# A gated delta-rule attention chain and a soft-MoE layer on one core: 64-row and 64-column array tiles, fixed key and query slots, 128-token outputs, a new instruction order

## The chip, the cores and the metric

The kernel runs on one core of one Trainium2 chip. A core has a matrix engine (PE, with weight loads shown apart as PEld), a vector engine (DVE), a scalar engine (ACT), GpSimd (POOL) and a DMA-issuing engine (SP). Each engine works through its own queue in order and waits on semaphores. PE writes to PSUM, which has 8 banks of 512 fp32 columns on 128 partitions; ACT and DVE copy ("evict") results from there to SBUF.

The metric is the device time of one execution in microseconds (us). Before the change it is 337.9 us, the median of three runs (336.04 to 340.29).

## The reference, cut to what matters

```python
# 4 batches x 8 heads, 768 tokens, head size 48
k_n = k / (norm(k) + 1e-06)
for t in range(S):
    y[:, :, t] = einsum('bhd,bhde->bhe', q[:, :, t], state)
    v_old = einsum('bhde,bhd->bhe', state, k_n[:, :, t])
    state = state + beta_t * einsum('bhd,bhe->bhde', k_n[:, :, t], v[:, :, t] - v_old)
x = y.transpose(0, 2, 1, 3).reshape(3072, 384)
logits = x @ phi                       # 32 slots: 8 experts x 4
d = softmax(logits, over tokens)
slot_input = d.T @ x
h = relu(slot_input[e] @ w1[e])        # 384 -> 1024
slot_out[e] = h @ w2[e]                # 1024 -> 384
c = softmax(logits, over slots)
out = c @ slot_out
```

## The kernel before, in words

**Chunks.** The 768 tokens are cut into 12 chunks of 64. The sequential recurrence inside a chunk is replaced by matrix products: with the Gram matrix of the keys, a 64x64 triangular system is inverted for each of the 32 heads, and the state is carried from chunk to chunk. Two batches' halves of the 32 heads sit on partitions 0-63 and 64-127 (index `r`); the 16 heads of a half are 8 pairs `j` with two members `c`.

**Work of one chunk n.** `load` brings K, Q and V (L414), K and V in ten DMAs each, Q in two. K and Q are padded from 48 to 64 columns per head by a memset (L420). `turn` transposes K and Q in 128x128 blocks on PE (L472) and evicts them into `KQ[n]` (L285 on ACT or L287 on DVE, the two copies of the helper `copy`). `prep` multiplies keys with keys and queries, the Gram products (L501, 48 rows contracted, 64x128 out), which are masked and spread (L509, L514, L524, L537). For each pair of chunks `invert` inverts 16x16 diagonal blocks elementwise (L559 to L617, its products and differences L281 on DVE or POOL). For each chunk `join` extends the inverse to 32 and to 64 by four PE products (L671, 64x64 stationary, 16 or 32 moving columns for each j, r) with evictions and corrections between (L681, L687/L689, L698, L708). `step` carries the state: `ks` = keys times state (L759), the difference with the scaled V (L765), `w` = inverse times difference (L776), interleaved with the previous chunk's attention product `mau` (L720), eviction to U, `sup` = state update (L803, accumulated in the fixed two-bank tile `pS`), and its eviction `sev` into the other state buffer (a 48-partition copy for each c, one on ACT, one on DVE, each reading both banks). `query` (L729) applies the old state to the queries. `route` transposes the output (L838); `pair` computes, for two chunks, the logits (L856), running softmax statistics, the slot sums (L891) and the combine weights (L900 to L920).

**After the last chunk** come the merge (L985 to L1009), the expert layers (L1025, L1041, L1058), the slot outputs (L1064, L1065), and the combination with the token weights (L1078): 24 groups of four products, each 64 tokens wide, one 384-column eviction and one 192 KB DMA (L1084) for each group. The weights `w1` and `w2` (25 MB) stream into SBUF during the second half (L964, L975), wherever earlier tiles have become free.

**Order and places.** The order of all operations, the engine of each that has a choice, and the SBUF and PSUM addresses are written out by hand in three tables, `ORDER`, `ALTS` and `PLACE`. They were made by a planner that is not part of the kernel; the durations in the calls of `pl.op` are its inputs and are not used when the kernel is built.

Of the kernel before, what the change touches and what calls it, by code (L numbers as in the profile page):

```python
# [10 lines left out]
AX = mybir.AxisListType  # L11
ALU = mybir.AluOpType
# [60 lines left out]
]  # L73
PLACE = [
# [126 lines left out]
def kernel(  # L201
# [108 lines left out]

    ident = lambda: A(cident)
    col1 = lambda c: A(cm0)[:, c:c + 1]
    M0, M1, NM0, NM1, LO, HI, NLO, NHI = [partial(col1, c) for c in range(8)]
    XMSK = lambda qq: A(cxm)[:, qq:qq + 1]

    pperm = pl.buf(1, psum=True)
# [799 lines left out]
```

## Time and profile before

| | |
|---|---|
| median of three runs | 337.9 us |
| the profiled execution | 337.52 us, of which the span from first to last instruction 335.8 us |
| mean PE clock granted over the span | 0.859 |
| PE idle until the first transposes (L472) | 17.0 us |
| first Gram products (L501) | 22.6 us |
| first spread for the inversion (L559) | 36.0 us |
| first `w` (L776) | 78.6 us |
| first expert product (L1025) | 290.3 us |
| last combination product (L1078) ends | about 327.5 us |
| HBM read, written | 39.5 MB, 4.7 MB |

Times inside a profile count from the first instruction. "x32" behind a PE line counts records: an fp32 matmul leaves two, an fp32 transpose one. The granted clock is a share of full speed; in this trace it is only ever 1.0 or 0.5, and it changes at multiples of 3.41 us from each other.

### The profile page before, as it was taken

How to read it: one execution, taken by the hardware profiler on the slowest of the kernel's cores; microseconds unless marked ns; L12 is line 12 of the kernel's file. 1: busy time of each engine (PE TensorE's matmuls, PEld its weight loads, DVE VectorE, ACT ScalarE, POOL GpSimd, SP SyncE). 2: the span in 40 equal slices, each digit the busy share in tenths (PEclk: the TensorE clock that was granted, in tenths of full speed). 3: DMA queues.
4: the chain of work that ended last, by engine and by line, in shares of the span. 5: the costliest groups of instructions: out<-in, count | busy, mean ns of one | idle time of the engine just before them, and what ended most of it. 6: DMA issues, size and time to landing. Idle time of an engine off the chain costs nothing.

```text
span 335.8 us, 14727 instructions
## 1 busy us (share of the span) xinstructions
PE 271.8 (81%) x6348; PEld 228.4 (68%) x6348; DVE 216.2 (64%) x570; ACT 130.6 (39%) x296; POOL 147.1 (44%) x257
## 2 busy tenths in 40 slices
PE   0086577898968798999899897997879699899990
PEld 0075466788967688888799676787759687336780
DVE  2264898669877585796768878478775465544360
ACT  1025437445615434463652413565433223130132
POOL 7060578134537465126662666272342622160110
PEclk9999658555969996999957998797978979999996
DMA  8976655430016646133111956367395957994287
GB/s 118 139 120 100 101 85 88 69 72 3 8 22 114 120 83 118 27 54 51 33 23 55 188 142 173 103 177 193 97 322 175 322 171 248 356 378 165 74 271 224
DMA packets 77697, 45.16 MB, mean 134 GB/s; under 512 B 60064, under 2 KB 70160, under 8 KB 77632
## 3 DMA queue, kind: packets, MB, share of 16 engines
q1 hardware_dynamic: 66304, 26.49, 34.8%
q0 software_dynamic: 6128, 15.31, 16.8%
q10 hardware_dynamic: 5200, 2.41, 2.8%
q8 instruction: 50, 0.82, 1.0%
q14 instruction: 15, 0.12, 0.1%
HBM read 39.47 MB, written 4.72 MB: 132 GB/s over the span
## 4 chain that ended last, share of the span: by engine, by line
PE 53%; DVE 21%; DMA 8%; issue 7%; ACT 5%; POOL 4%; SPq 1%; DVEq 0%; POOLq 0%; ACTq 0%
PE pb L671 11%; PE pb L501 7%; DVE sb L281 5%; PE pb L472 5%; PE pb L776 4%; PE pb L759 4%; DMA sb<-in_k_dram 4%; PE pb L1058 3%; PE pb L803 3%; PE pb L1025 3%; POOL sb L281 3%; PE pb L729 3%; PE pb L1078 3%; DMA sb<-in_v_dram 2%; PE pb L838 2%
## 5 line engine op out<-in xcount | busy, mean ns | idle before, releaser
L285 ACT ACTIVATE sb<-pb 128x512 f32<-128x512 f32 (+5 forms) x125 | 69.0, 578 | 132.7 <-PE pb L472 38.1
L281 POOL TENSOR_TENSOR sb<-sb 128x256 f32<-128x256 f32 (+10 forms) x108 | 62.6, 587 | 102.3 <-DVE sb L281 46.5
L671 PE MATMUL pb<-sb 64*64 64x16 f32 (+1 forms) x1536 | 62.9, 228 | 7.8 <-DVE sb L287 3.7
L671 PEld LDWEIGHTS pb<-sb 64*64 64x64 f32 x1536 | 59.2, 156 | 14.7 <-issue 8.6
L472 PE MATMUL pb<-sb 128*128 128x128 f32 x192 | 37.7, 350 | 23.7 <-DVE sb L330 17.0
L281 DVE TENSOR_TENSOR sb<-sb 128x120 f32<-128x120 f32 (+9 forms) x137 | 47.6, 351 | 9.8 <-POOL sb L281 4.8
L287 DVE COPY sb<-pb 128x384 f32<-128x384 f32 (+5 forms) x62 | 34.9, 573 | 26.1 <-PE pb L803 5.1
L472 PEld LDWEIGHTS pb<-sb 128*128 128x128 f32 x192 | 28.4, 179 | 28.6 <-issue 20.6
L501 PE MATMUL pb<-sb 48*64 48x128 f32 x768 | 35.0, 332 | 7.4 <-DVE sb L287 2.8
L501 PEld LDWEIGHTS pb<-sb 48*64 48x64 f32 x768 | 29.2, 168 | 10.0 <-ACT sb L285 5.6
L776 PE MATMUL pb<-sb 64*64 64x48 f32 x768 | 28.9, 234 | 4.4 <-DVE sb L765 3.0
L776 PEld LDWEIGHTS pb<-sb 64*64 64x64 f32 x768 | 27.0, 149 | 6.9 <-DVE sb L765 3.1
L720 PE MATMUL pb<-sb 64*64 64x48 f32 x768 | 27.2, 226 | 1.5 <-issue 1.5
L720 PEld LDWEIGHTS pb<-sb 64*64 64x64 f32 x768 | 25.3, 142 | 0.9 <-issue 0.8
L759 PE MATMUL pb<-sb 128*64 128x96 f32 x352 | 20.3, 278 | 3.2 <-DVE sb L287 1.8
L975 POOL DMA_DIRECT2D sb<-in_moe_w_dram x32 | 17.4, 546 | 11.8 <-PE pb L1025 7.7
L509 ACT ACTIVATE sb<-pb,sb 128x128 f32<-128x128 f32 x48 | 16.6, 366 | 15.1 <-DVE sb L537 7.9
L537 DVE TENSOR_TENSOR sb<-pb,sb 128x512 f32<-128x512 f32 x16 | 11.0, 688 | 17.5 <-ACT sb L509 7.7
L759 PEld LDWEIGHTS pb<-sb 128*64 128x64 f32 x352 | 18.2, 160 | 4.8 <-ACT sb L285 2.1
L729 PE MATMUL pb<-sb 128*64 128x96 f32 x352 | 17.6, 255 | 0.4 <-DVE sb L765 0.2
L414 POOL DMA_DIRECT2D sb<-in_k_dram x25 | 13.9, 567 | 8.8 <-DVE sb L429 8.8
L803 PE MATMUL pb<-sb 64*48 64x48 f32 x704 | 13.6, 228 | 4.7 <-issue 3.6
(139 smaller groups left out, 389.0 us busy)
## 6 DMA issues: line engine op xcount, KB each, us to landing
sb<-in_moe_w_dram SPq DMA_DIRECT2D x32, 256.0 KB, 5.1
sb<-in_moe_w_dram POOLq DMA_DIRECT2D x32, 192.0 KB, 5.4
sb<-in_moe_w_dram SPq DMA_DIRECT2D x32, 192.0 KB, 5.1
sb<-in_moe_w_dram POOLq DMA_DIRECT2D x16, 256.0 KB, 5.5
sb<-in_q_dram SPq DMA_DIRECT2D x13, 192.0 KB, 4.3
out_dram<-sb SPq DMA_DIRECT2D x10, 192.0 KB, 2.4
out_dram<-sb ACTq DMA_DIRECT2D x10, 192.0 KB, 3.5
sb<-in_k_dram SPq DMA_DIRECT2D x19, 96.0 KB, 3.5
```

What stands on the lines that cost most here:

```text
L281: ENG[e].tensor_tensor(*a, **kw)
L285: nc.scalar.activation(o, i, ACT.Copy)
L287: V.tensor_copy(o, i)
L472: nc.tensor.transpose(A(ps)[:, 0, P * j:P * j + P], A(src)[:, x:x + P], ident())
L501: mm(A(ps)[ha(r), c, P * j4:P * j4 + P], x[hd(c), j, r, 0:64], x[hd(c), j, r])
L671: mm(A(ps)[ha(r), 0, w * j:w * j + w], stat()[ha(r), 64 * j:64 * j + 64], mov()[ha(r), w * j:w * j + w])
L720: mm(pv(pY)[ha(1 - r), j // 4, j % 4, c], A(at)[ha(r), 512 * c + 64 * j:512 * c + 64 * j + 64], hv(u)[ha(r), j, c], start=first and c == 0 ...
L729: mm(A(pY)[ha(1 - r), j // 4, 96 * (j % 4):96 * (j % 4) + 96], kqv(KQ[n])[:, j, r, 1], Sv(n)[:, j, r], start=j % 4 == 0)
L759: mm(A(pR)[ha(r), j // 4, 96 * (j % 4):96 * (j % 4) + 96], kqv(KQ[n])[:, j, r, 0], Sv(n)[:, j, r])
L776: mm(pv(pW)[ha(r), j // 4, j % 4, c], A(Zs[n])[ha(r), 512 * c + 64 * j:512 * c + 64 * j + 64], hv(R)[ha(r), j, c])
L803: mm(A(pS)[hd(c), r, D * j:D * j + D], hv(Kb[n])[ha(r), j, c], hv(U)[ha(r), j, c], start=n == 0 and j == 0)
L975: ENG[q].dma_start(out=A(t)[:, Dm * x:Dm * x + Dm], in_=s[:, 2 * tp + x])
```

## The change

- `join` (L671): each product streams 64 moving columns in place of 16 or 32, the same columns repeated 4 or 2 times; the result takes 64 columns for each j, and the readers pick the first 16 or 32.
- Gram (L501): 64 rows are contracted in place of 48 (the pads are zero). `sup` (L803): the stationary tile has 64 columns in place of 48. `KQ` keeps keys and queries in two halves.
- K and Q have 8 and 4 fixed slots of 1,024 columns, used in turn. The pads are zeroed once for each slot ahead of the loads (12 memsets) and not for each load (24).
- 11 of the 24 `w1` tiles are placed in K and Q slots that are done with, and one `w2` tile in the last.
- The state is laid out by r first. `sev` copies one bank for each engine, as two 48-partition copies of 384 columns, in place of one 768-column copy that reads both banks.
- `invert`: the norms are three operations with a separate copy of the diagonal; each column step is two operations, product and difference, which may run on different engines.
- `pair`: sums come out of the exponentials (`accum_out`), so three DVE operations for each pair are gone; the exponential of the combine weights is four ACT calls of 32 columns in place of one of 128.
- The combination works on 128 tokens: 12 groups of four products (32 rows, 128 stationary columns, 192 moving), a 768-column eviction, and four 96 KB DMAs for each group.
- `ORDER`, `ALTS` and `PLACE` are new.

```diff
-    def load(src, n, split, pad):
-        W = 64 if pad else D
-        t = pl.buf(16 * W)
+    NK, NQ = 8, 4
+    kslot, qslot = [[fixed(1024) for _ in range(x)] for x in (NK, NQ)]
+    for i in range(NK):
+        pl.tag = ("pad", i)
+        for t in ([kslot[i]] + ([qslot[i]] if i < NQ else [])):
+            pl.op([("POOL", 0.32), ("DVE", 0.28)], None, lambda e, t=t: ENG[e].memset(
+                A(t).rearrange("p (x d) -> p x d", x=16)[:, :, D:], 0.0), w=[t])
...
+    def load(src, n, pad):
+        t = kslot[n % NK] if pad else pl.buf(KW)
...
-        if pad:
-            pl.op([("POOL", 0.32), ("DVE", 0.28)], None, lambda e: ENG[e].memset(
-                A(t).rearrange("p (x d) -> p x d", x=16)[:, :, D:], 0.0), w=[(t, 1)])
...
+    def load_q(n):
+        t = qslot[n % NQ]
...
-    kqv = lambda t: A(t).rearrange("p (j r a t) -> p j r a t", j=8, r=2, a=2)
+    kqv = lambda t: A(t).rearrange("p (a j r t) -> p j r a t", j=8, r=2, a=2)
...
-                            x = A(KQ[n]).rearrange("p (j r f) -> p j r f", j=8, r=2)
-                            mm(A(ps)[ha(r), c, P * j4:P * j4 + P], x[hd(c), j, r, 0:64], x[hd(c), j, r])
+                            x = kqv(KQ[n])
+                            mm(A(ps)[ha(r), c, P * j4:P * j4 + P].rearrange("p (a t) -> p a t", a=2),
+                               x[ha(c), j, r, 0], x[ha(c), j, r])
...
-            def go(e):
-                p = A(pr)[:, 0:n].rearrange("p (x i k) -> p x i k", x=2 * X, k=m)
-                sh = [P, 2 * X, w, m]
-                tt(e, p, blk(tb, j, j + 1, 0, m).broadcast_to(sh),
+            def mul(e):
+                tt(e, p(), blk(tb, j, j + 1, 0, m).broadcast_to(sh),
                    blk(lb, j, j + 1, j + 1, 16).rearrange("p x a i -> p x i a").broadcast_to(sh), op=ALU.mult)
+            pl.op(both, None, mul, r=[lb, tb], w=[pr], dp=True)
+
+            def sub(e):
                 t = blk(tb, j + 1, 16, 0, m)
-                tt(e, t, t, p, op=ALU.subtract)
+                tt(e, t, t, p(), op=ALU.subtract)
+            pl.op(both, None, sub, r=[pr], w=[tb], dp=True)
...
-                        mm(A(ps)[ha(r), 0, w * j:w * j + w], stat()[ha(r), 64 * j:64 * j + 64], mov()[ha(r), w * j:w * j + w])
+                        m = mov()[ha(r), w * j:w * j + w].unsqueeze(1).broadcast_to([64, RJ // w, w])
+                        mm(A(ps)[ha(r), 0, RJ * j:RJ * j + RJ].rearrange("p (a t) -> p a t", t=w), stat()[ha(r), 64 * j:64 * j + 64], m)
...
-                            mm(A(pS)[hd(c), r, D * j:D * j + D], hv(Kb[n])[ha(r), j, c], hv(U)[ha(r), j, c],
+                            mm(A(pS)[ha(c), r, D * j:D * j + D], A(Kb[n]).rearrange("p (j c d) -> p j c d", j=8, c=2)[ha(r), j, c], hv(U)[ha(r), j, c],
...
-            for c in H2:
-                def sev(e, c=c):
-                    o = A(nz).rearrange("p (j r c d) -> p r j c d", j=8, r=2, c=2)[hd(c), :, :, c]
-                    i = A(pS)[hd(c), :, 0:8 * D].rearrange("p r (j d) -> p r j d", d=D)
-                    copy(e, o, i)
+            for r in H2:
+                def sev(e, r=r):
+                    for c in H2:
+                        o = A(nz).rearrange("p (r j c d) -> p r j c d", j=8, r=2, c=2)[hd(c), r, :, c]
+                        copy(e, o, A(pS)[hd(c), r, 0:8 * D].rearrange("p (j d) -> p j d", d=D))
...
-            nc.scalar.activation(A(d), A(Lc), ACT.Exp, bias=A(nm))
+            nc.scalar.activation(A(d), A(Lc), ACT.Exp, bias=A(nm), accum_out=A(ls))
...
+        def ce():
+            for x in range(4):
+                nc.scalar.activation(A(Eg)[:, 32 * x:32 * x + 32], A(pN)[:, 0, 32 * x:32 * x + 32], ACT.Exp,
+                                     bias=A(cmx)[:, x:x + 1], accum_out=A(smv)[:, x:x + 1])
...
+    done = qslot + [kslot[x % NK] for x in (N - 1, *range(N - NK, N - 2))]
...
-            w1b[e, kk] = t = pl.buf(F)
+            w1b[e, kk] = t = done.pop(0) if done else pl.buf(F)
...
+        for g2 in range(NG // 2):
+            for z in H2:
+                po, ob = pl.buf(2, psum=True), pl.buf(2 * Dm)
+
+                def comb(po=po, z=z, g2=g2, so=so):
+                    for x in H2:
+                        for b in H2:
+                            p0 = 32 * (2 * z + b)
+                            g = 2 * g2 + x
+                            mm(A(po)[:, b, HD * x:HD * x + HD], A(cT)[p0:p0 + 32, P * g:P * g + P], A(so)[p0:p0 + 32])
```

More of the change, by code (lines that the diff above doesn't have):

```diff
@@ L163, in buf, with op @@
         return Buf(self, size, **kw)
-    def op(self, eng, dur, fn, r=(), w=(), after=(), bus=0.0, rec=0, hold=(), nd=1, dp=False, skip=None):
+    def op(self, eng, dur, fn, r=(), w=(), after=(), bus=0.0, rec=0, hold=(), nd=1, dp=False, skip=None, act=0):
         o = Op(eng if dur is None else [(eng, dur)], fn if dur is None else (lambda e: fn()))
-        o.nd, o.dp, o.skip = nd, dp, skip
+        o.nd, o.dp, o.skip, o.act = nd, dp, skip, act
         o.src, o.tag, o.bus, o.rec, o.soft = fn, self.tag, bus, rec, [x for x in self.soft if x is not None]
@@ L312 @@
     col1 = lambda c: A(cm0)[:, c:c + 1]
-    M0, M1, NM0, NM1, LO, HI, NLO, NHI = [partial(col1, c) for c in range(8)]
+    M0, M1, NM0, NM1, HI, LO, NHI, NLO = [partial(col1, c) for c in range(8)]
     XMSK = lambda qq: A(cxm)[:, qq:qq + 1]
@@ L399, in load @@
+    def load(src, n, pad):
+        t = kslot[n % NK] if pad else pl.buf(KW)
         s = src.rearrange("b h s d -> s (b h) d")
         d = lambda: A(t).rearrange("p (x d) -> p x d", x=16)[:, :, 0:D]
-        parts = []
         for r in H2:
             h0 = 16 * (1 - r)
-            if not split:
-                parts.append((64 * r, 64, slice(0, 16), n * C, slice(h0, h0 + 16)))
-                continue
-            parts.append((64 * r, 64, slice(0, 16, 2), n * C, slice(h0, h0 + 16, 2)))
+            parts = [(64 * r, 64, slice(0, 16, 2), n * C, slice(h0, h0 + 16, 2))]
@@ L409, in load @@
             for k in range(4):
                 parts.append((64 * r + 16 * k, 16, slice(1, 16, 2), n * C + 48 - 16 * k, slice(h0 + 1, h0 + 16, 2)))
-        def go(ps, e):
-            for p0, w, x, t0, hs in ps:
-                ENG[e].dma_start(out=d()[p0:p0 + w, x], in_=s[t0:t0 + w, hs])
-        h = len(parts) // 2
-        c = (2.6, 2.95, 2.5 if src is k and n < 2 else None) if split else (0.65, 0.86, 0.62 if n < 2 else None)
-        for r, ps in ((0, parts[:h]), (2, parts[h:])):
-            pl.op(dq(*c), None, partial(go, ps), w=[(t, r)], bus=0.0012 * 64 * 8, nd=h)
@@ L419, in load, with go @@
-        if pad:
-            pl.op([("POOL", 0.32), ("DVE", 0.28)], None, lambda e: ENG[e].memset(
-                A(t).rearrange("p (x d) -> p x d", x=16)[:, :, D:], 0.0), w=[(t, 1)])
+            def go(e, ps=parts):
+                for p0, w, x, t0, hs in ps:
+                    ENG[e].dma_start(out=d()[p0:p0 + w, x], in_=s[t0:t0 + w, hs])
+            pl.op(dq(2.6, 2.95, 2.5 if src is k and n < 2 else None), None, go, w=[(t, 2 * r)], bus=1.5, nd=5)
+        return t
+    def load_q(n):
+        t = qslot[n % NQ]
+        s = q.rearrange("b h s d -> s (b h) d")
+        d = lambda: A(t).rearrange("p (x d) -> p x d", x=16)
+        for r in H2:
+            pl.op(dq(0.67, 0.86, 0.75 if n < 2 else None), None, lambda e, r=r: ENG[e].dma_start(
+                out=d()[64 * r:64 * r + 64, :, 0:D], in_=s[n * C:n * C + C, 16 * (1 - r):16 * (2 - r)]), w=[(t, 2 * r)], bus=1.5)
@@ L553, in invert @@
         part = lambda t, i: A(t)[:, GS * i:GS * i + 1024]
-        pl.op(pop(GS * X)[:1], None, lambda e: ENG[e].memset(A(tb), 0.0), w=[tb])
+        pl.op([("POOL", 1.0), ("DVE", 1.05)], None, lambda e: ENG[e].memset(A(tb), 0.0), w=[tb])
         for i, g in enumerate(gs):
@@ L561, in invert, with norm1, norm2 @@
             pl.op("DVE", 1.25, spread, r=[Gd[g]], w=[(lb, i)])
-        y, y1, n4, sq = [pl.buf(32 * X) for _ in range(4)]
+        y, y1, n4, sq, mt = [pl.buf(32 * X) for _ in range(5)]
         dg = lambda t: A(t).rearrange("p (i f) -> p i f", f=GS)[:, :, 0:1024:33]
         v = lambda t: A(t).rearrange("p (i k) -> p i k", k=32)
-        def norms():
-            q = 1.0 - 3.02e-4
+        hq = 1.0 - 3.02e-4
+        def norm1():
             V.tensor_scalar(v(y).bitcast(I32), dg(lb).bitcast(I32), 0.5, float(0x1FBD1DF5), op0=ALU.mult, op1=ALU.add)
             V.reciprocal(A(sq), A(y))
-            V.scalar_tensor_tensor(v(sq), dg(lb), q, v(sq), op0=ALU.mult, op1=ALU.mult)
-            V.scalar_tensor_tensor(A(y1), A(y), q, A(sq), op0=ALU.mult, op1=ALU.add)
+            V.scalar_tensor_tensor(v(sq), dg(lb), hq, v(sq), op0=ALU.mult, op1=ALU.mult)
+            V.scalar_tensor_tensor(A(y1), A(y), hq, A(sq), op0=ALU.mult, op1=ALU.add)
+        pl.op("DVE", 1.02, norm1, r=[lb], w=[y, y1, sq], dp=True)
+        def norm2():
             V.reciprocal(A(sq), A(y1))
@@ L574, in norms, with norm3 @@
             V.scalar_tensor_tensor(A(n4), A(y1), 4e-6, A(sq), op0=ALU.add, op1=ALU.add)
+        pl.op("DVE", 0.82, norm2, r=[lb, y1], w=[n4, sq], dp=True)
+        def norm3():
             V.tensor_tensor(A(sq), A(n4), A(n4), op=ALU.mult)
@@ L577, in norms @@
             g0 = 32 * gs[0]
-            V.tensor_tensor(dg(tb), A(cbb)[:, g0:g0 + 32 * X].rearrange("p (i k) -> p i k", k=32), v(sq), op=ALU.mult)
-        pl.op("DVE", 1.7 if X == 1 else 2.5, norms, r=[lb, cbb], w=[n4, sq, tb, y, y1], dp=True)
+            V.tensor_tensor(A(mt), A(cbb)[:, g0:g0 + 32 * X], A(sq), op=ALU.mult)
+        pl.op("DVE", 0.82, norm3, r=[n4, cbb], w=[sq, mt], dp=True)
+        pl.op([("ACT", 0.22), ("DVE", 0.2), ("POOL", 0.3)], None, lambda e: nc.scalar.activation(dg(tb), v(mt), ACT.Copy) if e == "ACT" else ENG[e].tensor_copy(
+            dg(tb), v(mt)), r=[mt], w=[tb], dp=True)
         def scale(e):
-            o = blk(lb, 0, 16, 0, 16)
-            m = dg(tb).rearrange("p i (x t) -> p (i x) t", x=2) if X == 1 else None
             for i in range(X):
                 o = blk(lb, 0, 16, 0, 16)[:, 2 * i:2 * i + 2]
-                m = part(tb, i)[:, 0:1024:33].rearrange("p (x t) -> p x t", x=2)
+                m = A(mt)[:, 32 * i:32 * i + 32].rearrange("p (x t) -> p x t", x=2)
                 tt(e, o, o, m.unsqueeze(2).broadcast_to([P, 2, 16, 16]), op=ALU.mult)
-        pl.op([("DVE", 0.7 * X - 0.08 * (X - 1))], None, scale, r=[tb], w=[lb], dp=True)
+        pl.op([("DVE", 0.7 * X - 0.08 * (X - 1))], None, scale, r=[mt], w=[lb], dp=True)
         pr = pl.buf(128 * X)
@@ L624, in blocks @@
         return A(b).rearrange("p (s j i c) -> p s c j i", s=2, c=2, j=8)[:, s]
+    RJ = 64
     def join(n):
@@ L659, in mask @@
             return go
-        pl.op([("DVE", 0.78), ("POOL", 1.42), ("ACT", 1.1)], None, mask(Gd[g], s1, True), r=[(Gd[g], 2 * s), (Gd[g], 2 * s + 1), cs1, cm0], w=[s1], dp=True)
-        pl.op([("ACT", 0.88), ("DVE", 0.78), ("POOL", 1.42)], None, mask(td, s2, False), r=[td, cm0], w=[s2], dp=True)
+        pl.op([("DVE", 0.78), ("POOL", 1.45), ("ACT", 1.25)], None, mask(Gd[g], s1, True), r=[(Gd[g], 2 * s), (Gd[g], 2 * s + 1), cs1, cm0], w=[s1], dp=True)
+        pl.op([("ACT", 0.95), ("DVE", 0.55), ("POOL", 1.88)], None, mask(td, s2, False), r=[td, cm0], w=[s2], dp=True)
         def madd(e):
@@ L689, in wide @@
                     V.tensor_scalar(zv()[:, :, :, z], Z(), M1() if z else M0(), None, op0=ALU.mult)
-            pl.op([("ACT", 0.72), ("DVE", 0.72)], None, wide, r=[(zd, s), cm0], w=[(zs, z)], dp=True)
+            pl.op([("ACT", 0.76), ("DVE", 0.49)], None, wide, r=[(zd, s), cm0], w=[zs], dp=True)
         def zbadd(e):
@@ L783, in step @@
             Yb[n - 1] = pl.buf(KW)
-        chain[n] = pl.op("PE", t_pe(128, 16.2) if old else t_pe(64, 29.6), w(old), r=[Zs[n], R] + (old[1:3] if old else []),
+        chain[n] = pl.op("PE", t_pe(128, 15.0) if old else t_pe(64, 29.6), w(old), r=[Zs[n], R] + (old[1:3] if old else []),
                          w=[pW] + ([old[0]] if old else []), rec=128 if old else 64,
-                         hold=[U] + ([Yb[n - 1]] if old else []))
+                         hold=[U] + ([Yb[n - 1]] if old else []), act=1536 if old else 768)
         if old:
@@ L824, in au @@
                             mau(old, j, c, r)
-            pl.op("PE", t_pe(64, 29.6), au, r=old[1:3], w=[pY], rec=64, hold=[Yb[n]])
+            pl.op("PE", t_pe(64, 29.6), au, r=old[1:3], w=[pY], rec=64, hold=[Yb[n]], act=768)
             yev(n, pY)
@@ L870, in ex @@
         def ex():
-            nc.scalar.activation(A(d), A(Lc), ACT.Exp, bias=A(nm))
+            nc.scalar.activation(A(d), A(Lc), ACT.Exp, bias=A(nm), accum_out=A(ls))
             if old is not None:
                 nc.scalar.activation(A(al), A(df), ACT.Exp)
-        pl.op("ACT", 0.4 if old is None else 0.62, ex, r=[Lc, nm, df], w=[d, al])
+        pl.op("ACT", 0.45 if old is None else 0.67, ex, r=[Lc, nm, df], w=[d, al, ls])
         run["m"], run["l"] = nm, ls
-        def den():
-            V.tensor_reduce(A(ls), A(d), axis=AX.X, op=ALU.add)
-            if old is not None:
-                V.scalar_tensor_tensor(A(ls), A(lold), A(al), A(ls), op0=ALU.mult, op1=ALU.add)
-        pl.op("DVE", 0.5, den, r=[d, al] + ([lold] if lold else []), w=[ls])
+        if old is not None:
+            pl.op("DVE", 0.2, lambda: V.scalar_tensor_tensor(A(ls), A(lold), A(al), A(ls), op0=ALU.mult, op1=ALU.add),
+                  r=[al, lold], w=[ls])
         pD = pl.buf(1, psum=True)
-        pl.op("PE", 0.3, lambda: nc.tensor.transpose(A(pD)[:, 0, 0:P], A(d), ident()), r=[d, cident], w=[pD])
+        pl.op("PE", 0.3, lambda: nc.tensor.transpose(A(pD)[:, 0, 0:P], A(d), ident()), r=[d, cident], w=[pD], act=128)
         pl.op(ev(P), None, lambda e: copy(e, A(dN), A(pD)[:, 0, 0:P]), r=[pD], w=[dN])
@@ L928, in get_k @@
                 pl.soft = [chain.get(2 * gs[0] - 5)]
-                Kb[n] = load(k, n, True, True)
+                Kb[n] = load(k, n, 1)
         for g in gs:
@@ L933, in get_k @@
                 pl.soft = [chain.get(2 * gs[0] - 5)]
-                Qb[n] = load(q, n, False, True)
+                Qb[n] = load_q(n)
                 pl.soft = []
@@ L946 @@
         pl.soft = [chain.get(n - 3)]
-        Vb[n] = load(v, n, True, False)
+        Vb[n] = load(v, n, 0)
         pl.soft = []
@@ L968 @@
         for tp in range(NFC // 2):
-            w2b[e, tp] = t = pl.buf(2 * Dm)
+            w2b[e, tp] = t = last.pop() if last and e == E - 1 else pl.buf(2 * Dm)
             pl.tag = ("w2", e)
@@ L1026, in prod @@
                            A(w1b[4 * qq + j, kk])[:, f * HF:f * HF + HF], start=kk == 0)
-            pl.op("PE", 2.6, prod, r=[slb] + [w1b[4 * qq + j, kk] for j in range(4) for kk in range(NKT)], w=[ph], rec=24)
+            pl.op("PE", 2.6, prod, r=[slb] + [w1b[4 * qq + j, kk] for j in range(4) for kk in range(NKT)], w=[ph], rec=24, act=3072)
             def relu(e, f=f, ph=ph):
@@ L1067 @@
         pl.tag = ("out", h)
-        for y in H2:
-            for b in H2:
-                for g2 in range(NG // 2):
-                    po, ob = pl.buf(1, psum=True), pl.buf(Dm)
-                    def comb(po=po, y=y, b=b, g2=g2, so=so):
-                        for x in H2:
-                            for s in H2:
-                                p0 = 32 * (2 * s + b)
-                                t0 = P * (2 * g2 + x) + 64 * y
-                                mm(A(po)[ha(s), 0, HD * x:HD * x + HD], A(cT)[p0:p0 + 32, t0:t0 + 64], A(so)[p0:p0 + 32])
-                    pl.op("PE", 0.35, comb, r=[(cT, 2 * g2), (cT, 2 * g2 + 1), so], w=[po], rec=8, hold=[ob])
-                    pl.op(ev(Dm), None, lambda e, po=po, ob=ob: copy(e, A(ob), A(po)[:, 0, 0:Dm]), r=[po], w=[ob])
-                    def put(e, ob=ob, y=y, b=b, g2=g2, h=h):
-                        r0 = (2 * y + b) * S + 2 * P * g2
-                        ENG[e].dma_start(out=out[r0:r0 + 2 * P, HD * h:HD * h + HD].rearrange("(x p) d -> p x d", p=P),
-                                         in_=A(ob).rearrange("p (x d) -> p x d", x=2))
-                    pl.op(dq(0.45, 0.74, 0.48), None, put, r=[ob], bus=0.7)
@@ new lines, with put @@
+        for g2 in range(NG // 2):
+            for z in H2:
+                po, ob = pl.buf(2, psum=True), pl.buf(2 * Dm)
[5 more added lines that the diff above has]
+                            mm(A(po)[:, b, HD * x:HD * x + HD], A(cT)[p0:p0 + 32, P * g:P * g + P], A(so)[p0:p0 + 32])
+                pl.op("PE", 0.45, comb, r=[(cT, 2 * g2), (cT, 2 * g2 + 1), so], w=[po], rec=8, hold=[ob], act=384)
+                pl.op(ev(2 * Dm), None, lambda e, po=po, ob=ob: copy(
+                    e, A(ob).rearrange("p (b f) -> p b f", b=2), A(po)[:, :, 0:Dm]), r=[po], w=[ob])
+                for b in H2:
+                    def put(e, ob=ob, z=z, b=b, g2=g2, h=h):
+                        o = out.rearrange("(y b g s t) d -> b g s y t d", y=2, b=2, g=NG, s=2)
+                        for x in H2:
+                            ENG[e].dma_start(out=o[b, 2 * g2 + x, z][:, :, HD * h:HD * h + HD],
+                                             in_=A(ob)[:, Dm * b + HD * x:Dm * b + HD * x + HD])
+                    pl.op(dq(0.85, 1.45, 0.95), None, put, r=[ob], bus=0.7, nd=2)
```

111 lines of the change are left out of this document (56 added, 55 removed), and 184 rows, old and new, of tables (ORDER, PLACE).

## The prediction

> **What bounds the kernel now.** I read the page's first two parts, then the engines' busy time by stretches of one granted clock, then the chain that ended last, then the first 30 us in order of time.
>
> ```profile
> span 335.8 us, 14727 instructions
> ...
> PE 271.8 (81%) x6348; PEld 228.4 (68%) x6348; DVE 216.2 (64%) x570; ACT 130.6 (39%) x296; POOL 147.1 (44%) x257
> ...
> PE   0086577898968798999899897997879699899990
> ...
> PEclk9999658555969996999957998797978979999996
> ...
> PE 53%; DVE 21%; DMA 8%; issue 7%; ACT 5%; POOL 4%; SPq 1%; DVEq 0%; POOLq 0%; ACTq 0%
> ```
>
> PE is the busiest engine and carries 53% of the chain, and its clock row falls to 5 in the middle of the span, where the PE row stands at 8 and 9. So I cut the span where the clock changes (stretch, length, busy time of PE, PEld, DVE, ACT, POOL, then clock, DMA share, GB/s):
>
> ```profile
> 36.48:50.13 13.65, 9.26 (x64) 7.85 (x64) 12.38 (x42) 5.69 (x15) 8.00 (x15) 0.50 0.57 85
> 56.96:84.27 27.31, 24.05 (x350) 21.70 (x351) 20.92 (x56) 13.42 (x34) 10.03 (x14) 0.50 0.31 54
> 101.33:128.64 27.31, 22.14 (x826) 20.20 (x824) 18.93 (x44) 11.29 (x22) 16.15 (x30) 1.00 0.64 108
> 135.47:166.19 30.72, 28.16 (x811) 24.61 (x810) 24.74 (x63) 16.92 (x38) 11.79 (x26) 1.00 0.26 44
> 166.19:179.84 13.65, 13.65 (x258) 12.72 (x256) 8.62 (x24) 6.30 (x14) 7.01 (x9) 0.50 0.10 17
> ```
>
> The clock is at half in nine stretches between 36.48 and 272, 88.8 us in all; PE is busy for 78.9 us of them and DVE for 59.4. In the rest of that stage, 146.8 us, PE is busy for 124.3 us (85%) and DVE for 113.5 (77%). The chain shows what half a clock costs (start, length, piece):
>
> ```profile
> 64.45 1.79 PE pb L501 x30
> 66.23 1.63 PE pb L671 x32
> ...
> 219.53 1.08 PE pb L501 x32
> ...
> 258.35 1.05 PE pb L671 x32
> ...
> 277.44 2.00 PE pb L720 x64
> ...
> 320.89 5.08 PE pb L1078 x99
> ```
>
> Thirty Gram records (L501) take 1.79 us at 64 and thirty-two take 1.08 at 219, 0.565 of it per record; thirty-two L671 records take 1.63 at 66 and 1.05 at 258, 0.644. I use 0.60.
>
> When does the clock fall? Not when PE is idle: it is busy throughout 168 to 180 at 0.50. I counted for each 3.41 us the moving columns of all PE records, weighted by the share of the 128x128 array that their tile fills (transposes at half weight, which separates best). The windows before a fall, and those that stay low, hold at most 1,246 such columns; those before a rise, and those that stay high, hold at least 1,057, but for two (870 and 946). L671 with 16 moving columns on a quarter of the array keeps PE busy and fills next to nothing.
>
> **Array fill (the main term).** I recounted the same windows with 64 columns in L671, 64 rows in L501 and 64 columns in L803. The windows before three falls go from 1,163 to 1,955 (before 56.96), 759 to 1,521 (before 128.64) and 1,246 to 2,067 (before 166.19), clear of the boundary; those three stretches are 47.8 us of the 88.8. In the others windows of 732 to 1,067 stay (94.5, 203.7, 227.6, 248.1), so some falls remain. At full clock the 78.9 us of PE work become 78.9 x 0.60 = 47.3, and the stage's PE work 124.3 + 47.3 = 171.6.
>
> What the fill costs: the trace has no 64x64 product with 64 columns. The nearest rows are L720 alone with 48 columns (277.44: 2.00 us for 64 records, 31 ns) and L501 with 128 (34 ns); L671 itself takes 33 with 16 or 32. So 0 to 3 ns for each of 1,536 records, 0 to 4.6 us; nothing is gained, since the stationary tile is the same. I take 1 ns (48 columns is nearer than 128): 1.5 us. [...] L803 goes from 48 to 64 stationary columns: 0.92 us for 64 records now (102.06 on the chain, 14.4 ns); the interleaved L776/L720 pass has 64-column tiles at 15.6 ns (2.0 us for 128). 704 x 1.2 ns = 0.9 us, between 0 and 3.3 (in proportion to columns). L501's rows cost nothing: its records already load 64 columns and stream 128.
>
> PE work of the stage is then 174.0 us; at the 85% that it reaches today at full clock, 205.4. Four remaining falls of the shortest length in the trace (3.41 us, 92% busy, 40% of it lost) add 5: 210.4 in place of 235.5, **-25 us**. DVE must fit beside it: 172.9 us now in this stage, less some 10 (pair's three reductions and differences 6 x 0.85 = 5; half-masks of L655, ten on DVE now and four after, at 0.68 = 4; fewer L524, 6 x 0.30 = 1.8; POOL's and ACT's queues take those moved), 163 in 210 is 77%, what it reaches now.
>
> **Start.** Time order of the first 30 us (start, length, engine, line; idle time before it in brackets):
>
> ```profile
> 14.67 1.09 DVE L420 MEMSET sb<- 128x256 f32 x4 [10.70 <-DMA sb<-in_k_dram]
> ...
> 16.06 2.77 POOL L414 DMA_DIRECT2D sb<-in_k_dram  x5 [8.81 <-DVE sb L429]
> ...
> 17.02 1.94 PE L472 MATMUL pb<-sb 128*128 128x128 f32 x8 [17.02 <-DVE sb L330]
> ...
> 22.64 3.69 PE L501 MATMUL pb<-sb 48*64 48x128 f32 x64 [1.38 <-DVE sb L420]
> ```
>
> Since 3.97 us DVE's queue stood at a pad memset (L420) of a tile whose load was under way: idle 10.7 us. Behind it lay the other pads, on which the next K loads (POOL at 16.06, idle 8.81) and the Gram products (released by L420) waited. The new order puts the memsets ahead of the loads. The queues after the change show the first K half on SP and the other on POOL, five DMAs each, where SP now issues all ten up to 8.06 us and the last lands at 14.3 (chain: 7.75, 6.56 us of DMA); PE begins with Q, which ACT issues at 0.80 (6.3 us to landing). So transposes can start at some 8 us in place of 17.0, and the work from there to the first spread (19 us now, 14 of it PE) follows. The loads set a limit: 17 us carried 128 GB/s, and two chunks of K and Q (786 KB) need 6 us of it. Gain between 3 (only K's landing moves) and 11; I take **-8**, near the 9 by which the transposes move. The price is 0.3 us: the first load waits for one memset (272 ns). If the loads are late after all, PE waits for DMA where it waits for DVE now.
>
> **State chain.** `sev` is 803 ns on ACT and 954 on DVE for 768 columns; 384 columns are 490 and 553, twice that 980 and 1,106. +0.17 us in each of 11 steps, all on the way to the next `ks`: **+2** (0 if another product fills PE meanwhile). Two engines reading a bank's halves cost nothing today: 128 partitions x 768 take 807 and 954 on one engine alone.
>
> **Tail.** L1078 goes from 192 records to 96, at 51 ns now (5.08 us for 99). A 128-column tile with 192 moving columns is not in the trace: at 51 ns it saves 4.9 us of PE work, at twice that nothing. But the DMA engines are 1.03 busy from 324 to 330, and 2.36 MB must still go out after the last slot output, in 24 issues where there were 12. I take **-1.5**, from -4 to +2.
>
> **At nothing:** the split norms and columns of `invert` (the same DVE and POOL passes, one 32-column copy of 0.2 us more per pair of chunks), four ACT calls for one (ACT is 39% busy; if that cover is gone, +0.9 us per pair), `w1` in done slots (K9's slot comes free two steps before L1025; if late, PE waits there).
>
> **Sum**, against the profiled execution (337.5; the median is 337.9): 337.5 - 25 - 8 + 2 - 1.5 = **305 us**.
>
> **The rivals.** *DVE takes PE's place.* DVE is 91% busy from 36.48 to 50.13 and works 33.9 us in the three stretches. If that work stays bunched, they shrink only to 33.9 / 0.91 = 37.2, -10.6, and the other falls stay: 337.5 - 10.6 - 7.5 = 319. Against it: the average of 77%, and work taken off DVE. Chance 0.20.
>
> *The clock does not follow the fill.* Then L671's columns only cost: 337.5 + 3 (1.5 and 0.9 us, more at half clock) - 7.5 = 333. Against it: the separation above. [...] Chance 0.09.
>
> *The fixed Q slots starve PE.* A load of Q(n) may start only after Q(n-4) is transposed, and the queues after the change hold Q loads that wait for PE, on SP ahead of K and V loads and on POOL ahead of `invert`'s products. A load takes 4.3 to 5.0 us to land; if eight chunks each wait for one plus its 0.6 us of issue, and the array empties meanwhile: 8 x 6 = 48 us, 353. It decides from 5 us per chunk on (305 + 40 = 345). For it: the trace has such waits for Q (55.94, 3.65 us on the chain). Against: the transposes of Q(n-4) lie two pairs of chunks back, and a chunk takes some 17 us. Chance 0.07.
>
> **How the numbers follow.** My forecast, 288 to 316, 0.59; DVE-bound 0.20; no clock effect 0.09; starved 0.07; below 288 (PE over 90% busy at full clock) 0.05. The likeliest gives 305. Its unknown costs add up to some +10 and -12. A range of 288 to 330 takes in the DVE case and leaves out 0.05 below and about 0.15 above. A change of 2% (331.1 and 344.7) is about what a measurement of this kernel tells from none. Faster: 0.59 + 0.20 + 0.05 + a sliver of the no-clock case = 0.85; same 0.08; slower 0.07.
>
> **What would show it.** Right: mean clock above 0.93, no stretch at half longer than 7 us after 36, L671 at 1.0 to 1.1 us for 32 records, first L501 before 16 us and first spread before 30, half-clock time in the middle under 30 us. Wrong: a clock near 0.86 with L671 filled (no clock effect), DVE over 85% busy and PE waiting for L281 or L287 (DVE), PE idle behind DMA at the transposes (Q slots), L671 above 40 ns a record (the fill costs).

## The result, and the profile after

The kernel after takes 377.7 us (median of four runs, 376.6 to 379.0), the kernel before beside it 339.1 us: 1.117 times as long, 95% interval 1.107 to 1.127. Ratios compare executions within 1.5% of the fastest of their kernel, medians take all. The forecast was 305. The profiled execution has a span of 377.2 us where before had 335.8.

First the page of the kernel after: span and busy time, then the 40 slices of 9.4 us (PE, its granted clock, DMA engines) and the chain by engine. Lines have other numbers in the kernel after: L472, L501, L559, L671, L891, L1025, L1058, L1078 and L1084 of before are its L480, L509, L568, L694, L914, L1051, L1084, L1103 and L1111.

```profile
span 377.2 us, 14572 instructions
...
PE 255.2 (68%) x6252; PEld 210.9 (56%) x6252; DVE 201.2 (53%) x526; ACT 139.4 (37%) x365; POOL 157.6 (42%) x278
...
PE   2575738798889889999888995979699902500000
...
PEclk9998558999999999999999999699899965555555
DMA  6957435432407144375345499669962131221221
...
PE 45%; DVE 15%; DMA 13%; ACT 8%; issue 5%; POOL 3%; SPq 3%; ACTq 1%; POOLq 0%; DVEq 0%
```

Two halves are to be seen. Up to slice 31 the clock row is nearly all 9, where before it fell to 5 again and again. From slice 32 (some 300 us) PE has next to nothing to do, the clock is at half, and the DMA row stands at 1 to 3. Something slow goes on there that keeps the DMA engines neither busy nor idle.

Next, some of PE's instructions and the first spread (L568) of the kernel after in order of time (start, length, engine, line; idle time before it in brackets), the last of them the last slot product:

```profile
6.51 1.94 PE L480 MATMUL pb<-sb 128*128 128x128 f32 x8 [6.51 <-DMA sb<-in_q_dram]
...
14.73 1.99 PE L509 MATMUL pb<-sb 64*64 64x128 f32 x32
...
27.67 1.25 DVE L568 STREAM_TRANSPOSE sb<-sb 128x1024 f32<-128x1024 f32 x1
...
263.31 0.85 PE L914 MATMUL pb<-sb 128*32 128x384 f32 x8
```

The first spread and the last slot products of before:

```profile
35.88 1.19 DVE L559 STREAM_TRANSPOSE sb<-sb 128x1024 f32<-128x1024 f32 x1
...
286.34 1.50 PE L891 MATMUL pb<-sb 128*32 128x384 f32 x16
```

The first transposes, Gram products and spread come 10.5, 7.9 and 8.2 us sooner than before (17.02, 22.64, 35.88).

Then stretches of the kernel after (length, busy time of PE, PEld, DVE, ACT, POOL, then clock, DMA share, GB/s), the last one from the tail:

```profile
34.70:58.60 23.90, 14.62 (x226) 12.90 (x228) 18.30 (x49) 9.92 (x28) 10.28 (x19) 0.51 0.43 73
58.60:234.00 175.40, 155.54 (x4708) 137.78 (x4705) 138.11 (x339) 92.63 (x224) 92.73 (x169) 1.00 0.49 115
...
318.00:324.00 6.00, 5.29 (x36) 4.68 (x38) 1.72 (x3) 0.95 (x2) 1.49 (x2) 0.50 0.14 47
```

One long stretch at half clock is left at the start; then 175 us pass at full clock with PE 89% busy. From the first spread to the end of the last slot product it takes 236.5 us (27.67 to 264.17) where before took 252.0 (35.88 to 287.83). In that stretch of the tail the DMA engines are 0.14 busy and carry 47 GB/s; from 304 to 377 as a whole it is 0.20 and 57, with up to 88 in the stretches after POOL has issued. Before, the outputs went out at 316 GB/s with the engines 1.03 busy (324 to 330).

The end of the chain of waits of the kernel after (start, length, piece):

```profile
262.70 10.31 DMA sb<-in_moe_w_dram
...
273.15 5.36 PE pb L1051 x48
...
299.34 8.45 SPq L1111
...
307.85 9.36 DMA out_dram<-sb
...
317.82 0.33 ACT sb L1089
...
325.69 14.98 DMA out_dram<-sb
...
340.90 10.35 DMA out_dram<-sb
```

The output DMAs are most of the chain from 299 on, and they hold up more than themselves. ACT's queue has output DMAs (L1111) to issue ahead of the eviction L1089 that the second half of the outputs needs. ACT stood until an earlier output DMA had landed:

```profile
317.82 0.32 ACT L1089 COPY sb<-pb 128x192 f32<-128x192 f32 x1 [18.82 <-DMA out_dram<-sb]
```

PE waited 17.3 us for that eviction. In three cuts of the two spans: up to the first spread -8.2, from there to the end of the last slot product -15.5, from there to the end +65.1 (47.9 before, 113.1 after); together the +41.4 between 335.8 and 377.2.

The output DMAs (L1111) of the kernel after: duration of an issue on SP, minimum, median and maximum in ns, then us from issue to landing.

```profile
L1111 SPq DMA_DIRECT2D out_dram<-sb x26: 517/2208/8498, 292.8 to 367.8; - x26
...
DMA to landing us min/median/max: 4.9/8.5/10.9
```

The landings are those of the 16 DMAs of 96 KB that POOL issued; the profile has none for SP and ACT here. They take 8.5 us, and SP's queue stands for up to 8.5 us at one issue. Before, 192 KB landed in 3.9 us from POOL and 2.4 from SP, and an issue took SP 0.37.

### The profile page after: what moved, and what is told of

It is laid out like the page before. It is cut to its first block, busy times and chain, and to the rows that moved or that the text cites. A ratio compares the mean times of both kernels' runs of the same rounds, so it can differ in the third digit from the quotient of the medians.

```text
span 377.2 us, 14572 instructions
## 1 busy us (share of the span) xinstructions
PE 255.2 (68%) x6252; PEld 210.9 (56%) x6252; DVE 201.2 (53%) x526; ACT 139.4 (37%) x365; POOL 157.6 (42%) x278
## 4 chain that ended last, share of the span: by engine, by line
PE 45%; DVE 15%; DMA 13%; ACT 8%; issue 5%; POOL 3%; SPq 3%; ACTq 1%; POOLq 0%; DVEq 0%
DMA out_dram<-sb 9%; PE pb L694 9%; PE pb L509 5%; PE pb L480 5%; ACT sb L288 4%; PE pb L801 4%; DMA sb<-in_moe_w_dram 4%; PE pb L754 3%; PE pb L784 3%; SPq L1111 3%; PE pb L828 3%; PE pb L745 2%; PE pb L1084 2%; PE pb L1051 2%; DVE sb L284 2%
## 5 line engine op out<-in xcount | busy, mean ns | idle before, releaser
L284 POOL TENSOR_TENSOR sb<-sb 128x128 f32<-128x128 f32 (+10 forms) x119 | 63.0, 535 | 82.6 <-DVE sb L284 41.2
L694 PE MATMUL pb<-sb 64*64 64x64 f32 x1536 | 57.7, 228 | 12.3 <-POOL sb L284 5.6
L694 PEld LDWEIGHTS pb<-sb 64*64 64x64 f32 x1536 | 52.2, 142 | 19.0 <-POOL sb L284 8.2
L290 DVE COPY sb<-pb 48x384 f32<-48x384 f32 (+5 forms) x64 | 37.6, 599 | 42.0 <-PE pb L1103 10.8
L284 DVE TENSOR_TENSOR sb<-sb 128x120 f32<-128x120 f32 (+8 forms) x128 | 42.9, 342 | 15.2 <-POOL sb L284 13.0
L480 PE MATMUL pb<-sb 128*128 128x128 f32 x192 | 31.0, 305 | 16.0 <-DMA sb<-in_q_dram 6.5
L1111 POOL DMA_DIRECT2D out_dram<-sb x16 | 12.7, 800 | 60.6 <-ACT sb L288 59.9
L509 PE MATMUL pb<-sb 64*64 64x128 f32 x768 | 30.6, 310 | 7.1 <-ACT sb L288 5.5
L480 PEld LDWEIGHTS pb<-sb 128*128 128x128 f32 x192 | 23.2, 154 | 20.7 <-issue 11.7
L509 PEld LDWEIGHTS pb<-sb 64*64 64x64 f32 x768 | 25.7, 155 | 9.5 <-ACT sb L288 7.4
L801 PEld LDWEIGHTS pb<-sb 64*64 64x64 f32 x768 | 24.7, 135 | 5.6 <-DVE sb L790 2.2
L745 PEld LDWEIGHTS pb<-sb 64*64 64x64 f32 x768 | 24.4, 135 | 3.8 <-issue 3.7
L518 ACT ACTIVATE sb<-pb,sb 128x128 f32<-128x128 f32 x48 | 16.7, 370 | 12.5 <-PE pb L509 7.3
L784 PEld LDWEIGHTS pb<-sb 128*64 128x64 f32 x352 | 15.3, 137 | 3.9 <-ACT sb L288 2.4
L754 PEld LDWEIGHTS pb<-sb 128*64 128x64 f32 x352 | 16.0, 144 | 2.0 <-ACT sb L518 0.5
```

Of the source, the lines that this page charges most:

```text
L284: ENG[e].tensor_tensor(*a, **kw)
L290: V.tensor_copy(o, i)
L480: nc.tensor.transpose(A(ps)[:, 0, P * j:P * j + P], A(src)[:, x:x + P], ident())
L509: mm(A(ps)[ha(r), c, P * j4:P * j4 + P].rearrange("p (a t) -> p a t", a=2), x[ha(c), j, r, 0], x[ha(c), j, r])
L694: mm(A(ps)[ha(r), 0, RJ * j:RJ * j + RJ].rearrange("p (a t) -> p a t", t=w), stat()[ha(r), 64 * j:64 * j + 64], m)
L745: mm(pv(pY)[ha(1 - r), j // 4, j % 4, c], A(at)[ha(r), 512 * c + 64 * j:512 * c + 64 * j + 64], hv(u)[ha(r), j, c], start=first and c == 0 ...
```

## The experiments

**The destination of the output DMAs.** The combination by 128 tokens has partitions that count two blocks `y` of 64 tokens `t`, 1,536 rows apart. So a DMA's destination is a pattern of 2 x 64 x 192 elements with 2 outermost; before it was 128 x 2 x 192. The first kernel cuts the same bytes the other way:

```diff
-                        for x in H2:
-                            ENG[e].dma_start(out=o[b, 2 * g2 + x, z][:, :, HD * h:HD * h + HD],
-                                             in_=A(ob)[:, Dm * b + HD * x:Dm * b + HD * x + HD])
+                        for y in H2:
+                            ENG[e].dma_start(out=o[b, 2 * g2:2 * g2 + 2, z, y, :, HD * h:HD * h + HD].rearrange("x t d -> t x d"),
+                                             in_=A(ob)[ha(y), Dm * b:Dm * b + Dm].rearrange("p (x d) -> p x d", x=2))
```

> The kernel after, with each output DMA cut along y (64 tokens outermost, then the two groups x, then 192) where it was cut along x (two blocks y outermost, then 64 tokens, then 192); still 48 DMAs of 96 KB from the same tiles, everything ahead of them as it was. Theory (a DMA whose outermost dimension is 2 runs on 2 of the 16 DMA engines, and the output queue crawls at some 46 GB/s behind it): the outputs go out at some 300 GB/s again, the last slot output of the second half starts at about 302 where it started at 320, and the tail from there is the 15 us of before: 317 to 322 us. Rival (it is the number of issues, 48, or the products with 128 tokens, that make the tail slow): the DMAs keep landing after 8 to 9 us each one behind the other, 365 to 380.

Measured: 316.4 us (314.9 to 319.0), just under the expected range, 0.947 of before [0.935, 0.959]; again, on another chip, 319.0 us, 0.961 [0.947, 0.976] (expected: 

> e1_put_by_y once more, beside the next two on one chip: 312 to 320 us.

). The profiled span is 315.6 us, 61.6 less than after, and this edit is the only difference; 59 of them lie behind the last slot product (53.9 us in place of 113.1). Its output DMAs and a stretch of its tail, in two views:

```profile
L1111 SPq DMA_DIRECT2D out_dram<-sb x26: 595/608/1422, 291.2 to 311.1; - x26
...
DMA to landing us min/median/max: 2.2/3.0/4.2
```

```profile
300.00:306.00 6.00, 4.61 (x50) 3.30 (x49) 3.20 (x4) 1.62 (x2) 2.61 (x5) 1.00 0.76 200
```

The same 26 issues on SP are through in 21 us where they took 77. So neither their number nor the products with 128 tokens make the tail slow.

**A dose of it, on the kernel before.** Its 24 output DMAs of 192 KB are cut into 48 of 96 KB, first with 128 rows, then with the destination in 4 blocks of 32 rows and in 2 of 64 (a = 4, 2), so that only the outermost dimension and the order of the rows differ between the three:

```diff
-                        ENG[e].dma_start(out=out[r0:r0 + 2 * P, HD * h:HD * h + HD].rearrange("(x p) d -> p x d", p=P),
-                                         in_=A(ob).rearrange("p (x d) -> p x d", x=2))
+                        o = out[r0:r0 + 2 * P, HD * h:HD * h + HD].rearrange("(a x t) d -> x a t d", a=2, x=2)
+                        for x in H2:
+                            ENG[e].dma_start(out=o[x], in_=A(ob)[:, HD * x:HD * x + HD])
```

> The kernel before with its 24 output DMAs of 192 KB cut into 48 of 96 KB, each 128 rows of 192: the control for the next two. Theory (engines per DMA): still all engines, so only the issues are added, some of them beside other work: 334 to 343 us. Rival (48 issues are what makes the tail after slow): 360 or more.

> The control b_k16 with the destination of each DMA in 4 blocks of 32 rows (block outermost, blocks 64 rows apart), the same bytes and runs of 768 bytes; the rows of the output come out in another order. Theory (four DMA engines at 23 GB/s each, 95 GB/s, for the 3.9 MB that SP and ACT issue; from 315 on): 350 to 368 us. Rival (not the outermost dimension): within 2% of b_k16.

> The same with 2 blocks of 64 rows, as in the kernel after; the rows of the output come out in another order. Theory (two engines, 47 GB/s, 84 us for 3.9 MB from 315 on): 390 to 410 us, and DMA engines 0.12 to 0.16 busy in that stretch. Rival (not the outermost dimension): within 2% of b_k16.

Measured, one execution each: 334.5, 366.5 and 409.7 us, with the kernel before at 341.2 on that chip. A stretch of the tail of each, in that order (POOL issues nothing in the second and third):

```profile
318.00:324.00 6.00, 4.89 (x80) 3.75 (x74) 3.25 (x6) 1.59 (x4) 0.38 (x1) 1.00 0.77 239
```

```profile
352.00:358.00 6.00, 0.00 (x0) 0.00 (x0) 0.00 (x0) 1.25 (x3) 0.00 (x0) 0.50 0.27 93
```

```profile
340.00:346.00 6.00, 0.00 (x0) 0.00 (x0) 0.00 (x0) 0.53 (x2) 0.00 (x0) 0.50 0.14 47
```

With 4 outermost the rate is 93 GB/s at a DMA share of 0.27, with 2 it is 47 at 0.14: half the rate and half the share for half the outermost dimension, some 23 GB/s for each unit of it. Forty-eight issues cost nothing that shows (334.5 us beside 341.2). Of 16 engines these shares are 4.3 and 2.2, near the 4 and 2 that the expectations count. Which engines they are, and how a single DMA is spread over them, no run shows. SP and ACT together stay at 47 GB/s with 2 outermost while both have DMAs left to issue: SP's last issue is at 388.9 and ACT's at 396.7.

**POOL as the issuer.** All 48 output DMAs go to POOL, in the pattern of after and in that of the first experiment:

```diff
-                    pl.op(dq(0.85, 1.45, 0.95), None, put, r=[ob], bus=0.7, nd=2)
+                    pl.op([("POOL", 1.45)] * 3, None, put, r=[ob], bus=0.7, nd=2)
```

> The kernel after, its output DMAs in their shape with two blocks outermost, but all 48 issued by POOL. [...] Rival (the pattern itself is slow, whichever engines carry it): 365 or more, as after.

> e1_put_by_y (64 tokens outermost) with all 48 output DMAs issued by POOL, as e2b_put_on_pool did it with two blocks outermost. Theory (the 10.5 us that POOL's DMAs took to land in e2b_put_on_pool came from two engines for each): they land after 3 to 4 us, POOL no longer waits for its own earlier DMAs, and 48 issues of 0.6 us from 293 on, 29 us, set the end: 320 to 330 us. Rival (POOL's queue is slow by itself): landings of 8 us and more, 345 or more.

Measured: 368.5 us and 332.1 us. The landings of the two kernels:

```profile
DMA to landing us min/median/max: 4.4/10.5/12.0
```

```profile
DMA to landing us min/median/max: 2.1/2.2/3.2
```

The first came out where its rival has it, at 365 or more. With 2 outermost POOL carries some 75 GB/s (59 to 86 in stretches of 6 us from 312 to 354, at DMA shares of 0.30 to 0.46), more than the 47 of SP and ACT, but the tail is not bound by POOL's issues of 0.8 us each: 17 times POOL waited for an earlier output DMA, 19.5 us in all. With 64 outermost that wait is gone and the issues are bound as expected, 48 in 28.5 us, but the end is 2 us above the range since they began at 296 and not at 293. So the slow landings on POOL are the pattern's too. Why it carries only some 75 GB/s with 2 outermost, and how many engines one of its DMAs takes, no run tells.

**The fill of the array.** The kernel before gets the fill alone, first in L671, then in L501 and L803 as well; and the repaired kernel (e1_put_by_y) has it taken back in L694. The core of the edit to the kernel before:

```diff
-                        mm(A(ps)[ha(r), 0, w * j:w * j + w], stat()[ha(r), 64 * j:64 * j + 64], mov()[ha(r), w * j:w * j + w])
+                        m = mov()[ha(r), w * j:w * j + w].unsqueeze(1).broadcast_to([64, RJ // w, w])
+                        mm(A(ps)[ha(r), 0, RJ * j:RJ * j + RJ].rearrange("p (a t) -> p a t", t=w), stat()[ha(r), 64 * j:64 * j + 64], m)
```

> The kernel before with 64 moving columns in L671 alone (L501 and L803 as they were). Theory (the clock follows the fill, and L671 brings most of the columns): 30 to 55 us at half clock between 36 and 272 where the kernel before has 89, 322 to 331 us. Rival (the stationary tiles' 48 rows and columns count too as much): 60 us or more at half clock, 330 to 338.

> The kernel before with the array fill alone: 64 moving columns in L671, 64 stationary columns in L501 and in L803; order, places, pads, outputs as before. Theory (the clock follows the fill): the half-clock time in the main stage drops from 89 to 25 to 45 us, mean clock 0.92 to 0.97, 312 to 325 us. Rival (the clock does not follow the fill): three half-clock stretches of 13 and 27 us stay, 337 to 341 us.

> e1_put_by_y with the products of L694 at 16 and 32 moving columns again in place of 64 (the same number of records). Theory (the granted clock follows how much of the array the records fill): the half-clock stretches come back, some 40 to 70 us of them from 36 to 272, mean clock 0.87 to 0.92, and the time is 10 to 20 us over e1_put_by_y. Rival (the clock goes by something else that the change brought, such as the earlier start or the order): clock and time within 1% of e1_put_by_y.

Half-clock time is summed from the granted clock of 2 us stretches between 30 and 272 of the profiled execution (for the last kernel it is its longest, 330.1 us); ratios are to the kernel before on the same chip:

| kernel | at half clock, us | median, us | against before |
|---|---|---|---|
| before | 88.8 | 339.1 | |
| before, L671 filled | 47.9 | 329.9 | 0.984 [0.941, 1.026] |
| before, all three filled | 30.7 | 324.1 | 0.967 [0.945, 0.988] |
| after | 34.2 | 377.7 | 1.117 [1.107, 1.127] |
| after, repaired | 26.3 | 316.4 | 0.947 [0.935, 0.959] |
| after, repaired, L694 small | 64.9 | 324.9 | 0.969 [0.957, 0.982] |

The clock rows of the kernel before with all three filled, and of the repaired one with L694 small again:

```profile
PEclk9999759787989999999999999999999899999996
```

```profile
PEclk9999555569999998999589999999597999799995
```

The half-clock time follows the fill in both directions, whichever order and start the kernel has: from 88.8 to 30.7 us with the fill put in, from 26.3 to 64.9 with L694's taken back. How the fill is to be counted no run tests by itself, but two traces bear on it. Set each window of 3.41 us against the clock granted in the next one, and put the boundary where it separates best. The weighted columns of the prediction then leave 7 of the 91 windows of the kernel before on the wrong side; PE's busy time leaves 16, and the columns without the tile's share 17. With L694 small it is 5, 14 and 8 of 92. With L671 alone it falls as expected, but the time can't be told from before. With all three the time falls by 12.2 us (336.4 for before on that chip), as expected. Taking L694 back costs 8.5 us (322.8 to 330.1 against 314.9 to 319.0), which is short of the 10 to 20 expected. For the price I use all executions and not the profiled ones alone: 2 x (1 - mean clock) x span, averaged, is 88 us for before, 38 filled, 35 repaired and 68 with L694 small. So 12.2 / 50 = 0.24 and 8.5 / 33 = 0.26 us of time for each us at half clock.

**What is left in the repaired kernel.** Two changes to its end were tried: the output DMAs spread evenly over SP and POOL, and on top of that half of the bytes of `w2` left out (the second half of the outputs is made from the first half's columns).

```diff
-                    pl.op(dq(0.85, 1.45, 0.95), None, put, r=[ob], bus=0.7, nd=2)
+                    qe = ["SP", "POOL"][b] if (h, g2, z) != (0, 2, 1) else "ACT"
+                    pl.op([(qe, 0.85)] * 3, None, put, r=[ob], bus=0.7, nd=2)
...
-                    ENG[q].dma_start(out=A(t)[:, Dm * x:Dm * x + Dm], in_=s[:, 2 * tp + x])
+                    ENG[q].dma_start(out=A(t)[:, Dm * x:Dm * x + Dm // 2], in_=s[:, 2 * tp + x, 0:Dm // 2])
```

> e1_put_by_y with the output DMAs of each tile given half to SP and half to POOL (those of the last tile to ACT), where SP had 26 of 48 and its queue held back to back issues of 0.6 us from 291 to 311. Theory (after the repair the tail is bound by SP's issues): the last landing comes 3 to 4 us sooner, 311 to 314 us. Rival (the last copies set the end): within 1 us of f0_put_by_y_again.

> f1_put_queues with half of the bytes of each load of w2 (its first 192 of 384 columns; the second half of the outputs is made from them too), 6.3 MB less on the DMA engines. Theory (from 216 on the weights' stream bounds PE's start on L1051): the wait of 3 us before and within L1051 goes, and the end comes 3 to 6 us sooner than in f1_put_queues. Rival (the loads of w1 wait for their slots, not for the DMA engines): within 1 us of f1_put_queues.

Measured: 318.9 us (316.9 to 321.8), 319.0 beside it for the repaired kernel as it was, and 314.8 (314.3 to 314.9). The queues of the output DMAs were not the bound: with 22 issues in place of 26, SP's last one is at 310.7 in place of 311.1 (e1_put_by_y), and the time is the rival's. That the last copies set the end, as the rival has it, was not tried. The stream of the weights is a bound: with half of `w2` the time is 4.2 us shorter, as expected, and from the first expert product to the first product with `w2` (L1084) it takes 14.4 us in place of 16.5. The kernel before took 12.1 for that (L1025 to L1058). The way was not quite the expected one: the waits within L1051 that the profile puts down to the weights' DMAs stay (1.6 us and 1.5), and idle time of PE there without a named cause goes from 8.8 to 6.4.

The repaired kernel (e1_put_by_y, with or without the even queues) is the fastest that computes the reference: 0.95 to 0.96 of before.

## Why the prediction was wrong, point by point

**The step that failed** is the tail's: "in 24 issues where there were 12. I take -1.5, from -4 to +2". It priced the output DMAs by bytes and issues, at the rate that the old pattern reaches. I noted their number and size, not the pattern of a destination, and took the share of 1.03 for a property of the tail when it belonged to DMAs with 128 rows outermost. In place of -1.5 the tail took +65.1, and the pattern of the destination is 59 of it (113.1 against 53.9 us). The products themselves came out as priced: they run at 94 to 106 ns a record (sixteen in 1.50 us, eight in 0.85) in place of 51, and "at twice that nothing".

**The rivals** missed it too. The one on the slow side (Q slots) looked for queued DMAs among the loads; PE waited for Q once, 6.5 us, at the very start. DVE did not take PE's place over the stage: at full clock PE is 89% busy and DVE 79%. In patches it did: between 48 and 54 DVE is busy for 5.83 of 6 us and PE for 0.85, and in five of the 29 stretches of 6 us from 60 to 234 DVE is busy for 5.86 to 5.96 us and PE for less (72 to 78: 5.92 and 4.98).

**The clock.** That it follows the fill is shown by the table above, so the rival of 333 falls. How busy PE is does not tell the kernels apart: with L694 small PE is 86% busy from 27 to 274 and 64.9 us are at half clock, with it filled PE is 84% busy from 27 to 262 and 26.3 us are. The columns cost nothing that shows: records of L694 take 218 ns at the median where L671 took 219. Nor do the rows: L509 takes 269 ns at the median with 64 rows, as L501 did with 48.

**The size of the main term.** Main stage and `sev` together were to give -23 and gave -15.5. PE's share is as forecast: 200.0 us of work in the 236.5 are 85% (218.8 before). Mis-sized was the half-clock time left over, "four remaining falls of the shortest length", 13.7 us: 34.2 us stayed, some 23 of them from 34.7 to 58.6. The first fall of before (36.48) was never recounted, nor the last (268.58). In that early stretch of the kernel after PE has little to fill the array with: it is 61% busy. Mis-sized too was the price. The forecast's 25 us for 75.1 us less (88.8 to 13.7) are 0.33 for each, and the runs above give some 0.25. By that price, an estimate, the 54.6 us that went are worth 14 of the 15.5; the fill alone, put into the kernel before, gave 12.2. What the new order and the other edits add to that was not taken apart.

**The start** was right: -8 forecast, -8.2 measured, -9.4 in the repaired kernel. So were its signs: the first Gram products at 14.73 (forecast before 16) and the first spread at 27.67 (before 30). The signs for the clock, no stretch at half longer than 7 us and under 30 us in all, did not come.

**"At nothing".** The `w1` wait came where it was named ("if late, PE waits there"): from the first expert product (L1051) to the first product with `w2` (L1084) the repaired kernel takes 18.1 us, before 12.1, and the profile puts 3.9 us of waiting there down to the weights' DMAs. Two of these six go with half of `w2`'s bytes when the two kernels with even queues are compared, so the bytes are part of it; the rest was not taken apart. The split norms and the copies of `sev` (483 and 550 ns for 384 columns) were not tried alone.

**The sum with the failed step mended:** 335.8 - 9.4 (start) - 16.7 (main) + 6.0 (weights and the end) = 315.7, the repaired kernel's span but for rounding, where the forecast's terms would have given 303.3. Without the pattern the forecast's sign and its range of 288 to 330 would have held (316.4 us).

## What to carry to other kernels

When an edit changes which rows a tile holds, write out the source and destination pattern of every DMA that reads it, and look at the outermost size: a share of the DMA engines as low as the 0.14 and 0.27 of these runs (2 and 4 outermost), with a queue that never empties, is the sign in a profile. A microsecond at half clock is worth less than the 0.4 us that a busy PE loses in it (at full clock the records that the prediction compares took 0.565 and 0.644 of their time), here some 0.25; a likely reason, not tried by itself, is that other engines set a part of the pace. When a stage gets shorter, ask which transfers had been hidden behind it: here a part of the weights' loads was.

## What the runs showed of the hardware

- DMAs with 2 or 4 outermost on SP and ACT move 47 or 93 GB/s in all, at DMA shares of 0.14 and 0.27 (b_k2, b_k4), while both have more to issue. With 2 an issue on SP takes 2.2 us at the median and up to 8.5 (after; 0.6 at the median with 64 outermost, e1_put_by_y), and ACT stood 18.8 us before the eviction behind its own.
- On POOL the same pattern with 2 outermost lands in 10.5 us at the median and with 64 in 2.2, at the same 96 KB (e2b_put_on_pool, h1_by_y_on_pool).
- The clock row stays at half throughout the tail (304 to 377), where PE is busy for 7.5 us of 73, so the mean clock of 0.859, equal to before's, says nothing of the main stage (0.94).
- The half-clock time of one and the same kernel changes from one execution to the next: the kernel before had mean clocks from 0.845 to 0.909, which is 61 to 105 us at half clock as 2 x (1 - mean clock) x span, in 18 executions on two chips. The profile that the forecast was made from (0.859) shows one draw of it.
